# Two more trees for k's maximum, a new list of all steps, and the two-input chain carried on to batch 6

## The chip, the core and the metric

The kernel runs on one core of a Trainium2 chip. A core has five engines that work through queues of their own and wait for one another through semaphores: TensorE (PE, matrix products), VectorE (DVE), ScalarE (ACT), GpSimd (POOL) and SyncE (SP, which here only issues transfers). The metric is the device time of one launch in microseconds, as the median of several runs; lower is better.

## The reference

Attention with two softmaxes feeds a feed-forward block with a product in its middle. There are 8 batches of 8 heads, 576 tokens and 64 channels in each head; the feed-forward block has 4608 tokens, 512 channels and 1024 hidden columns.

```python
q_s = softmax(q, axis=-1)            # over the 64 channels, eps 1e-9 in the divisor
k_s = softmax(k, axis=2)             # over the 576 tokens
kv  = einsum('bhsd,bhse->bhde', k_s, v)
x   = einsum('bhsd,bhde->bhse', q_s, kv)   # then tokens x (heads * channels)
out = ((x @ w1) * (x @ w2)) @ w3 @ w_out
```

Each softmax subtracts its maximum before the exponential, as `np.max` and `np.exp` in the reference do.

## The kernel before, in words

`w3 @ w_out` is folded into one matrix first (`fold`): `w3t` transposes a block of w3 on TensorE, `w3T` copies it out of PSUM, `pf` multiplies it with w_out in two halves, `W3O` scales the result into SBUF. Fillers (`FILL`, line 350) keep TensorE busy at the start.

The eight batches of attention (`attention(b)`) each run these steps. For k: `kmx` is the maximum over the nine token groups that a partition holds; `cb` carries it across the partitions; `ksub` subtracts it (in two halves, by heads), `kexp` takes the exponential, `vc` casts v (batches 0 and 1 load v cast already), `kv` is the product, `kv2` divides by the sums and moves it out of PSUM. For q, in two parts of four and five token groups: `qmx` maximum, `qsub`, `qexp`, `qsm` sum, `qeps` and `qrc` (1e-9 added, reciprocal), `qn` product, then a transpose: `qt` and `qT` through TensorE for batches 0 and 1, `qd` by a transposing transfer from batch 2 on. `xm` and `xt` multiply both, `xs` and `xts` move the result to SBUF as x.

The feed-forward block (`chunk(c)`) takes the tokens of one batch at a time (chunks 0 to 7 the first 512, chunk 8 the last 64 of every batch). `up.1` and `up.0` are the products with w2 and w1, `bs` copies the first out of PSUM, `ab` multiplies both (VectorE), `down` multiplies with the folded matrix, `os` copies out, `st` stores. Chunks 0 and 1 are cut into two halves of 256 tokens. The number behind a name is batch or chunk, then half, block, or part: `up.0.0.1.2` is the w1 product of chunk 0, half 1, block 2.

The maximum `kmx` has two forms. `kmx_one` (line 481) is one reduce on VectorE for each half of the heads. `kmx_tree` (line 488) is four two-input maxima on whole tiles, 4, 2, 1 and 1 token groups wide. `TREES` (line 310) is the number of batches, from 0 on, that use the tree.

What runs on which engine is written out in `PICKS`, and the order on every engine in `ORDER`: the steps are emitted in that order, so each engine's queue is its share of the list. `LOADS` is the order of transfers issued by GpSimd, `LATE` of those by SyncE, which also issues `st` and `qd`. A load waits for the landing of the one eight places ahead of it in its queue, and for the buffer that it fills. PSUM is cut into rings: four banks for `up` (`pab`), two for `down` (`po`), two for attention (`att`). An `up` that finds its ring full waits for the `bs` or `ab` that frees the oldest bank.

Two-input steps of GpSimd and of VectorE (`pairs`, `kmx_tree`, `qeps` of VectorE, `vc` of GpSimd) are marked `port`. Among the first `LINKED` steps of the list, a marked step waits for the marked step ahead of it in the list if that one is on the other engine:

```python
if s["port"] and i < LINKED:
    assert got, name
    if held and held[0] != s["eng"]:
        link(got[0], held[1])
    held = s["eng"], got[-1]
```

Of the kernel before, what the change touches and what calls it, by code (L numbers as in the profile page):

```python
# [101 lines left out]
os.1.3 up.1.2.0.2 up.0.2.0.2 bs.2.0.2 qrc.3.0 ab.2.0.1 qn.3.0 kexp.3.0 up.1.2.0.3 ab.2.0.2  # L102
up.0.2.0.3 kmx.4.1 bs.2.0.3 kv.3 qd.3.0 up.1.2.0.4 ab.2.0.3 up.0.2.0.4 vc.5.0 vc.5.1 vc.4.1 vc.4.0
k.5 st.1.3 st.0.3 st.1.1 v.6 v.7 bs.2.0.4 kv2.3 os.1.2 up.1.2.0.5 ab.2.0.4 st.1.2 up.0.2.0.5
bs.2.0.5 qmx.4.0 xt.2 xm.3.1 xts.2.0 up.1.2.0.6 xts.2.1 ab.2.0.5 qsub.4.0 xs.3.1.1 xm.3.0 bs.2.0.6
xt.3 up.0.2.0.6 xts.3.1 xs.3.0.0 cb.4 up.1.2.0.7 xts.3.0 xs.3.0.1 up.0.2.0.7 xs.3.1.0 bs.2.0.7
ab.2.0.6 up.1.3.0.0 ksub.4.0 qexp.4.0 ab.2.0.7 down.2.0 kmx.5.1 bs.3.0.0 down.2.1 ksub.4.1 kexp.4.0
qmx.5.1 up.0.3.0.0 os.2.0 up.1.3.0.1 qsub.5.1 kexp.4.1 ab.3.0.0 down.2.2 qmx.5.0 bs.3.0.1 kmx.5.0
qsub.5.0 up.0.3.0.1 qeps.4.1 up.1.3.0.2 up.0.3.0.2 qrc.4.1 os.2.1 ab.3.0.1 qn.4.1 up.1.3.0.3 qsm.4.0
k.6 st.2.1 down.2.3 bs.3.0.2 qeps.4.0 ab.3.0.2 qexp.5.1 qd.4.1 up.0.3.0.3 qrc.4.0 qn.4.0 bs.3.0.3  # L110
st.2.0 up.1.3.0.4 qsm.5.1 kv.4 bs.3.0.4 ab.3.0.3 up.0.3.0.4 qd.4.0 qexp.5.0 os.2.2 up.1.3.0.5
ab.3.0.4 q.6 st.2.2 up.0.3.0.5 kv2.4 bs.3.0.5 qeps.5.1 up.1.3.0.6 os.2.3 qrc.5.1 ab.3.0.5 qn.5.1
up.0.3.0.6 st.2.3 bs.3.0.6 xm.4.0 ab.3.0.6 xm.4.1 xs.4.0.0 xt.4 up.1.3.0.7 xs.4.1.1 up.0.3.0.7
xs.4.1.0 bs.3.0.7 xs.4.0.1 ab.3.0.7 down.3.0 cb.5 down.3.1 os.3.0 xts.4.1 st.3.0 xts.4.0 kmx.6.0
ksub.5.0 up.1.4.0.0 os.3.1 down.3.2 bs.4.0.0 st.3.1 q.7 kmx.6.1 ksub.5.1 qd.5.1 up.0.4.0.0 kexp.5.0
up.1.4.0.1 qsm.5.0 up.0.4.0.1 bs.4.0.1 ab.4.0.0 qeps.5.0 up.1.4.0.2 kexp.5.1 ab.4.0.1 up.0.4.0.2
qrc.5.0 bs.4.0.2 qmx.6.1 qn.5.0 up.1.4.0.3 os.3.2 vc.6.0 up.0.4.0.3 st.3.2 ab.4.0.2 up.1.4.0.4
# [791 lines left out]
```

## Time and profile before

| | |
|---|---|
| median of 3 runs | 242.06 us (242.03 to 242.16) |
| the profiled execution | 242.07 us, of which the span is 240.3 us |
| granted TensorE clock | 1.00 |
| busy: TensorE, VectorE, ScalarE, GpSimd | 232.4, 182.0, 118.5, 110.2 us |
| transfers issued by SyncE, by GpSimd | 34.22 MB, 11.14 MB |

The span runs from the first to the last instruction of the profile. Each row of a timeline gives the start, the length, the engine (PEld is TensorE's loading of weights, which runs beside its products), the line of the kernel, the operation with the tiles it writes and reads, and, in brackets, how long the engine stood idle before it and what ended that wait. An instruction's length includes some 0.1 us in which the next one already runs, so the distance of starts tells what an instruction costs its engine. Times of matmul ends are modelled.

```profile
DVE  2949798989899899989689999997756335535530
```

This row has the busy tenths of VectorE in 40 slices of 6 us each.

### The profile page before, as it was taken

How to read it: one execution, taken by the hardware profiler on the slowest of the kernel's cores; microseconds unless marked ns; L12 is line 12 of the kernel's file. 1: busy time of each engine (PE TensorE's matmuls, PEld its weight loads, DVE VectorE, ACT ScalarE, POOL GpSimd, SP SyncE). 2: the span in 40 equal slices, each digit the busy share in tenths (PEclk: the TensorE clock that was granted, in tenths of full speed). 3: DMA queues.
4: the chain of work that ended last, by engine and by line, in shares of the span. 5: the costliest groups of instructions: out<-in, count | busy, mean ns of one | idle time of the engine just before them, and what ended most of it. 6: DMA issues, size and time to landing. Idle time of an engine off the chain costs nothing.

```text
span 240.3 us, 4954 instructions
## 1 busy us (share of the span) xinstructions
PE 232.4 (97%) x1987; PEld 121.0 (50%) x1987; DVE 182.0 (76%) x306; ACT 118.5 (49%) x187; POOL 110.2 (46%) x73
## 2 busy tenths in 40 slices
...
DVE  2949798989899899989689999997756335535530
...
GB/s 203 217 305 209 324 222 296 235 393 391 314 261 277 402 217 194 323 372 284 206 232 213 260 125 0 57 151 68 65 124 87 46 0 0 0 132 1 131 131 131
DMA packets 37894, 45.66 MB, mean 190 GB/s; under 512 B 15984, under 2 KB 22384, under 8 KB 37872
## 3 DMA queue, kind: packets, MB, share of 16 engines
q1 hardware_dynamic: 30080, 34.22, 50.3%
q0 software_dynamic: 7792, 11.14, 21.1%
...
## 4 chain that ended last, share of the span: by engine, by line
PE 83%; DVE 6%; DMA 6%; issue 2%; POOL 1%; ACT 1%; DVEq 0%; POOLq 0%
PE pab L768 50%; PE po L790 23%; DMA k<-in_k_dram 6%; PE po L805 3%; PE pkv L540 2%; PE po L452 2%; PE xm L654 2%; DVE ab L783 1%; DVE k L515 1%; DVE km L484 1%; PE qtp L621 1%; POOL w L402 1%; PE po L654 1%; DVE mx L506 1%; DVE kmx L493 1%
## 5 line engine op out<-in xcount | busy, mean ns | idle before, releaser
L783 DVE TENSOR_TENSOR ab<-pab,bsb 128x512 f16<-128x512 f32 x72 | 48.7, 682 | 24.0 <-PE pab L768 19.7
L768 PE MATMUL pab<-x,w2sb 128*128 128x512 f16 (+1 forms) x320 | 66.0, 337 | 0.0
L768 PE MATMUL pab<-x,w1sb 128*128 128x512 f16 (+1 forms) x320 | 65.9, 337 | 0.0
L323 ACT CAST bsb<-pab 128x512 f16<-128x512 f32 x59 | 34.5, 587 | 54.3 <-PE pab L768 53.9
L790 PE MATMUL po<-W3O,ab 128*128 128x512 f16 x256 | 59.7, 379 | 1.2 <-DVE ab L783 1.2
L768 PEld LDWEIGHTS <-w1sb 128*128 128x128 f16 x352 | 33.9, 98 | 27.6 <-DMA w1sb<-in_moe_w_dram 0.2
L768 PEld LDWEIGHTS <-w2sb 128*128 128x128 f16 x352 | 33.4, 98 | 27.6 <-issue 1.3
L790 PEld LDWEIGHTS <-ab 128*128 128x128 f16 x256 | 24.7, 98 | 30.6 <-DVE ab L783 1.9
L515 POOL TENSOR_TENSOR k<-k,cb 128x1152 f32<-128x1152 f32 x12 | 31.4, 2636 | 14.9 <-DVE cb L511 8.4
L574 POOL TENSOR_TENSOR q<-q,qm 128x1024 f32<-128x1024 f32 (+1 forms) x14 | 29.7, 2125 | 12.8 <-DVE qm L569 12.7
L606 POOL TENSOR_TENSOR en<-eq,qr 128x1280 f16<-128x1280 f16 (+1 forms) x12 | 25.8, 2159 | 20.7 <-DVE qr L599 20.7
L484 DVE TENSOR_REDUCE km<-k 128x128 f32<-128x1152 f32 x12 | 25.9, 2166 | 0.0
L569 DVE TENSOR_REDUCE qm<-q 128x20 f32<-128x1280 f32 (+1 forms) x16 | 21.3, 1342 | 3.6 <-DMA q<-in_q_dram 3.6
L523 ACT ACTIVATE ek<-k 128x1152 f16<-128x1152 f32 x16 | 18.5, 1163 | 9.5 <-POOL k L515 8.8
L323 ACT COPY osb<-po 128x512 f32<-128x512 f32 (+1 forms) x22 | 12.7, 576 | 20.6 <-PE po L790 14.1
L323 DVE COPY osb<-po 128x512 f32<-128x512 f32 (+1 forms) x15 | 10.0, 668 | 15.4 <-PE po L790 9.7
L587 DVE TENSOR_REDUCE qr<-eq 128x20 f32<-128x1280 f16 (+1 forms) x16 | 21.3, 1341 | 0.5 <-ACT eq L582 0.5
L582 ACT ACTIVATE eq<-q 128x1280 f16<-128x1280 f32 (+1 forms) x16 | 18.8, 1174 | 5.6 <-POOL q L574 3.8
L452 PE MATMUL po<-wosb,w3T 128*128 128x512 f16 x64 | 15.5, 379 | 0.7 <-DMA wosb<-in_moe_w_out_dram 0.4
L327 ACT ACTIVATE x<-xm 128x512 f16<-128x512 f32 x18 | 10.4, 608 | 4.6 <-PE xm L654 4.6
L323 DVE CAST bsb<-pab 128x512 f16<-128x512 f32 x13 | 8.9, 687 | 2.8 <-PE pab L768 2.3
L350 PE MATMUL po<-zero 128*128 128x512 f16 x31 | 9.2, 458 | 1.6 <-DVE zero L345 1.6
...
## 6 DMA issues: line engine op xcount, KB each, us to landing
...
q<-in_q_dram SPq DMA_DIRECT2D x6, 1152.0 KB, 6.8
v<-in_v_dram SPq DMA_DIRECT2D x6, 1152.0 KB, 10.0
k<-in_k_dram SPq DMA_DIRECT2D x5, 1152.0 KB, 6.8
k<-in_k_dram POOLq DMA_DIRECT2D x3, 1152.0 KB, 14.2
...
```

The lines of the kernel that those rows point to most:

```text
L323: return [(nc.scalar.copy if eng == "ACT" else engine[eng].tensor_copy)(out=out, in_=in_)]
L452: nc.tensor.matmul(st["pf", ft], lhsT=st["w3T", ft][:, gt, :], rhs=wosb[:, gt, :], start=(gt == 0), stop=(gt == N_FT - 1))
L484: dve.tensor_reduce(out=st["km", b][:, two(hp), :], in_=kb[:, two(hp), :, :].rearrange("p h j d -> p h d j"), axis=AX.X, op=ALU.max)
L515: return [engine[eng].tensor_tensor(out=kb[:, two(hp), :, :], in0=kb[:, two(hp), :, :], in1=st["cb", b][:, two(hp), None, :].broadcast_to( ...
L569: dve.tensor_reduce(out=st["qm", b][:, :, j], in_=qb[:, :, j, :], axis=AX.X, op=ALU.max)
L574: return [engine[eng].tensor_tensor(out=qb[:, :, j, :], in0=qb[:, :, j, :], in1=st["qm", b][:, :, j, None].broadcast_to([P, HH, n, D]), op ...
L582: nc.scalar.activation(out=st["eq", b, p], in_=qb[:, :, j, :], func=AF.Exp)
L587: dve.tensor_reduce(out=st["qr", b][:, :, slice(*PARTS[p])], in_=st["eq", b, p], axis=AX.X, op=ALU.add)
L606: return [engine[eng].tensor_tensor(out=st["en", b][:, j, :, :].rearrange("p j h d -> p h j d"), in0=st["eq", b, p], in1=st["qr", b][:, :, ...
L768: nc.tensor.matmul(st["p", one, c, sub, u][:, a * (t1 - t0):(a + 1) * (t1 - t0)], lhsT=w[:, ct, fb * P:(fb + 1) * P], rhs=x()[:, ct, t0:t1 ...
L783: dve.tensor_tensor(out=st["ab", c][:, nf * u:nf * u + nf, t0:t1], in0=cut(st["p", 0, c, sub, u]), in1=cut(st["bsb", c, sub, u]), op=ALU.mult)
L790: nc.tensor.matmul(st["po", c, tb], lhsT=st["ab", c][:, ft, tb * P:(tb + 1) * P], rhs=W3O[:, ft, :], start=(ft == 0), stop=(ft == N_FT - 1))
```

## The change

The change does four things. `TREES` goes from 2 to 4, so `kmx.2.0` and `kmx.3.0` are trees, and `kmx.2.1` and `kmx.3.1` fall away. `LINKED` goes from 350 to 559, which reaches into batch 6's products. `ORDER` and `PICKS` are written anew for every engine. `LOADS` and `LATE` follow: row 1 of w3 is loaded ahead of `k.0`, and `v.0` behind `w3.2` and `q.1.0`; SyncE's loads of batches 3 to 7 change places among themselves and with the stores.

```diff
-LINKED = 350
+LINKED = 559
 
 ORDER = """
-q.0.1 q.0.0 qmx.0.1 qsub.0.1 w3.3 w3.4 qexp.0.1 qmx.0.0 wo.0 wo.1 k.0 ident qsub.0.0 qexp.0.0 w3t.3
-w3t.4 w3t.5 w3T.3 qsm.0.1 w3T.4 qeps.0.1 qrc.0.1 w3.0 w3.1 pf.3.0 qn.0.1 pf.4.0 qt.0.16 pf.3.1 W3O.3
-w3T.5 pf.4.1 qt.0.8 w3.5 v.0 w3.2 q.1.0 qT.0.8 W3O.4 pf.5.0 w3t.0 k.1 w3T.0 pf.5.1 w2.0 W3O.5 w3t.1
-pf.0.0 qT.0.16 w3T.1 pf.0.1 W3O.0 w3t.7 w3T.7 pf.1.0 w3t.6 pf.7.0 pf.1.1 w1.0 qsm.0.0 qeps.0.0
-kmx.0.0 cb.0 ksub.0.1 kexp.0.1 w1.1 ksub.0.0 qrc.0.0 kexp.0.0 kv.0 qn.0.0 kv2.0 w3t.2 pf.7.1 qt.0.0
-w2.1 qmx.1.0 W3O.1 w3T.6 k.2 W3O.7 w3T.2 pf.6.0 w2.2 qT.0.0 xm.0.0 xs.0.0.1 qsub.1.0 w1.2 qexp.1.0
-kmx.1.0 pf.6.1 pf.2.0 pf.2.1 xs.0.0.0 xm.0.1 xs.0.1.0 xs.0.1.1 up.1.0.0.0 up.0.0.0.0 up.1.0.1.0
-bs.0.0.0 up.0.0.1.0 up.1.0.0.1 w2.3 qsm.1.0 qeps.1.0 ab.0.0.0 qrc.1.0 w1.3 up.0.0.0.1 cb.1 qn.1.0
-v.1 ksub.1.0 q.1.1 ksub.1.1 qt.1.0 W3O.2 bs.0.1.0 ab.0.1.0 up.1.0.1.1 up.0.0.1.1 bs.0.0.1 W3O.6
-qT.1.0 bs.0.1.1 ab.0.0.1 q.2 v.2 kmx.2.0 ab.0.1.1 xt.0 kexp.1.0 up.1.0.0.2 bs.0.0.2 up.0.0.0.2
-up.1.0.1.2 up.0.0.1.2 kmx.2.1 ab.0.0.2 cb.2 ksub.2.0 ksub.2.1 xts.0.0 xts.0.1 up.1.0.0.3 up.0.0.0.3
-bs.0.0.3 ab.0.0.3 down.0.0 kexp.1.1 bs.0.1.2 ab.0.1.2 kv.1 kv2.1 down.0.1 xm.1.0 qmx.1.1 xs.1.0.0
-os.0.0 kexp.2.0 xs.1.0.1 up.1.0.1.3 up.0.0.1.3 up.1.1.0.0 up.0.1.0.0 bs.0.1.3 kexp.2.1 qsub.1.1
-qmx.2.0 qsub.2.0 bs.1.0.0 os.0.1 qexp.1.1 qmx.2.1 ab.0.1.3 vc.2.1 vc.2.0 down.0.2 up.1.1.0.1
-qexp.2.0 qsub.2.1 ab.1.0.0 qsm.1.1 qeps.1.1 bs.1.0.1 up.0.1.0.1 up.1.1.0.2 kv.2 k.3 v.3 st.0.0 q.3
-qsm.2.0 qeps.2.0 qrc.1.1 qn.1.1 qexp.2.1 ab.1.0.1 up.0.1.0.2 up.1.1.0.3 up.0.1.0.3 qrc.2.0 kv2.2
-bs.1.0.3 os.0.2 qsm.2.1 qt.1.16 qt.1.8 qeps.2.1 bs.1.0.2 ab.1.0.3 qrc.2.1 qT.1.16 ab.1.0.2 qn.2.0
-down.0.3 qn.2.1 qT.1.8 xm.1.1 vc.3.0 xs.1.1.1 xs.1.1.0 q.4 down.1.0 qd.2.0 kmx.3.0 qd.2.1 qmx.3.0
-xt.1 vc.3.1 up.1.1.1.0 up.0.1.1.0 up.1.1.1.1 bs.1.1.0 up.0.1.1.1 up.1.1.1.2 xts.1.0 bs.1.1.1 os.1.0
-xts.1.1 kmx.3.1 ab.1.1.0 os.0.3 qmx.3.1 xm.2.0 qsub.3.0 qmx.4.1 ab.1.1.1 qsub.3.1 qsub.4.1
-up.0.1.1.2 down.1.1 xs.2.0.1 bs.1.1.2 k.4 st.0.1 v.5 v.4 st.0.2 xs.2.0.0 xm.2.1 xs.2.1.1 xs.2.1.0
-up.1.1.1.3 up.0.1.1.3 up.1.2.0.0 bs.1.1.3 qexp.3.1 ab.1.1.2 cb.3 ksub.3.0 ksub.3.1 up.0.2.0.0
-ab.1.1.3 kmx.4.0 bs.2.0.0 qexp.3.0 q.5 qsm.3.1 os.1.1 qexp.4.1 qsm.3.0 qeps.3.0 ab.2.0.0 qeps.3.1
-qrc.3.1 qn.3.1 qd.3.1 st.1.0 qsm.4.1 kexp.3.1 up.1.2.0.1 bs.2.0.1 up.0.2.0.1 down.1.2 down.1.3
...
+q.0.1 qmx.0.1 q.0.0 qsub.0.1 qmx.0.0 qexp.0.1 w3.3 w3.4 wo.0 wo.1 w3.1 ident qsub.0.0 w3t.3 w3T.3
+k.0 w3.0 w3t.4 qsm.0.1 qexp.0.0 qeps.0.1 qrc.0.1 w3T.4 w3t.5 pf.3.0 pf.4.0 qsm.0.0 qeps.0.0 pf.3.1
+W3O.3 w3.5 w3.2 q.1.0 qn.0.1 qt.0.8 pf.4.1 w3t.1 qrc.0.0 w3T.5 v.0 k.1 w2.0 qn.0.0 qt.0.16 pf.5.0
+w3T.1 W3O.4 qT.0.8 pf.5.1 kmx.0.0 cb.0 qt.0.0 w3t.0 W3O.5 ksub.0.1 w3T.0 pf.1.0 pf.1.1 pf.0.0 W3O.1
+ksub.0.0 w3t.7 pf.0.1 w3T.7 qT.0.0 qT.0.16 kexp.0.1 W3O.0 w3t.2 pf.7.0 w3t.6 w3T.2 qmx.1.0 kexp.0.0
+pf.7.1 w1.0 W3O.7 qsub.1.0 pf.2.0 w1.1 w2.1 k.2 w3T.6 kv.0 kv2.0 pf.2.1 qexp.1.0 xm.0.0 qsm.1.0
+xs.0.0.1 pf.6.0 pf.6.1 xs.0.0.0 qeps.1.0 xm.0.1 xs.0.1.0 up.1.0.0.0 xs.0.1.1 up.0.0.0.0 up.1.0.1.0
+w2.2 kmx.1.0 qrc.1.0 w1.2 cb.1 w2.3 w1.3 v.1 qn.1.0 bs.0.0.0 up.0.0.1.0 up.1.0.0.1 ab.0.0.0 W3O.2
+qt.1.0 ksub.1.0 q.1.1 up.0.0.0.1 bs.0.1.0 up.1.0.1.1 bs.0.0.1 ab.0.1.0 qT.1.0 xt.0 ab.0.0.1 bs.0.1.1
+kmx.2.0 up.0.0.1.1 up.1.0.0.2 ab.0.1.1 up.0.0.0.2 up.1.0.1.2 up.0.0.1.2 xts.0.0 xts.0.1 kexp.1.0
+bs.0.0.2 ab.0.0.2 up.1.0.0.3 up.0.0.0.3 bs.0.1.2 up.1.0.1.3 ksub.1.1 cb.2 q.2 kexp.1.1 ab.0.1.2
+up.0.0.1.3 v.2 W3O.6 bs.0.0.3 ab.0.0.3 kv.1 down.0.0 ksub.2.0 bs.0.1.3 kexp.2.0 kv2.1 ksub.2.1
+xm.1.0 os.0.0 xs.1.0.1 xs.1.0.0 qmx.1.1 ab.0.1.3 kexp.2.1 down.0.1 qmx.2.0 qsub.1.1 up.1.1.0.0
+up.0.1.0.0 up.1.1.0.1 up.0.1.0.1 qsub.2.0 vc.2.0 down.0.2 qmx.2.1 bs.1.0.0 qexp.1.1 os.0.1 vc.2.1
+qexp.2.0 ab.1.0.0 qsm.1.1 bs.1.0.1 qeps.1.1 qsm.2.0 qsub.2.1 os.0.2 qrc.1.1 qn.1.1 ab.1.0.1 qeps.2.0
+kv.2 up.1.1.0.2 up.0.1.0.2 up.1.1.0.3 kv2.2 qrc.2.0 up.0.1.0.3 qt.1.16 qt.1.8 down.0.3 qexp.2.1
+qsm.2.1 bs.1.0.3 bs.1.0.2 qn.2.0 qeps.2.1 ab.1.0.3 ab.1.0.2 qrc.2.1 st.0.0 k.3 q.3 v.3 st.0.2 qT.1.8
+qd.2.0 qn.2.1 st.0.1 qd.2.1 k.4 qT.1.16 xm.1.1 xs.1.1.0 xs.1.1.1 down.1.0 xt.1 qmx.3.1 up.1.1.1.0
+qmx.3.0 kmx.3.0 up.0.1.1.0 up.1.1.1.1 os.0.3 up.0.1.1.1 bs.1.1.0 bs.1.1.1 cb.3 qsub.3.0 down.1.1
+xts.1.1 xts.1.0 os.1.0 qexp.3.0 xm.2.0 ab.1.1.1 qsub.3.1 ab.1.1.0 xs.2.0.1 xs.2.0.0 up.1.1.1.2
+up.0.1.1.2 qsm.3.0 xm.2.1 qexp.3.1 xs.2.1.0 xs.2.1.1 bs.1.1.2 ab.1.1.2 qsm.3.1 up.1.1.1.3 up.0.1.1.3
+bs.1.1.3 ab.1.1.3 up.1.2.0.0 up.0.2.0.0 up.1.2.0.1 qeps.3.1 vc.3.0 kmx.4.0 bs.2.0.0 up.0.2.0.1
+ab.2.0.0 qeps.3.0 bs.2.0.1 qrc.3.0 ksub.3.1 ksub.3.0 kexp.3.0 q.4 kexp.3.1 up.1.2.0.2 up.0.2.0.2
+up.1.2.0.3 vc.3.1 os.1.1 qrc.3.1 ab.2.0.1 kmx.4.1 qmx.4.1 kv.3 down.1.2 up.0.2.0.3 qn.3.0 kv2.3 xt.2
+bs.2.0.3 bs.2.0.2 qmx.4.0 ab.2.0.2 os.1.2 st.0.3 v.4 q.5 qd.3.0 qn.3.1 up.1.2.0.4 down.1.3
+up.0.2.0.4 qsub.4.1 qd.3.1 qexp.4.1 ab.2.0.3 xts.2.1 xts.2.0 os.1.3 xm.3.0 xm.3.1 xt.3 bs.2.0.4
+qsm.4.1 ab.2.0.4 qeps.4.1 xts.3.0 xs.3.0.1 xts.3.1 xs.3.0.0 up.1.2.0.5 bs.2.0.5 xs.3.1.1 xs.3.1.0
+qsub.4.0 vc.4.0 cb.4 ksub.4.1 up.0.2.0.5 up.1.2.0.6 up.0.2.0.6 qexp.4.0 ab.2.0.5 ksub.4.0 up.1.2.0.7
+up.0.2.0.7 qrc.4.1 qmx.5.1 bs.2.0.6 ab.2.0.6 vc.4.1 k.5 st.1.1 up.1.3.0.0 up.0.3.0.0 st.1.3 qsm.4.0
+st.1.2 st.1.0 v.5 bs.2.0.7 qmx.5.0 ab.2.0.7 up.1.3.0.1 kexp.4.1 qeps.4.0 kexp.4.0 bs.3.0.0 qrc.4.0
+kmx.5.1 down.2.0 up.0.3.0.1 kv.4 kmx.5.0 qn.4.1 os.2.0 vc.5.1 bs.3.0.1 v.6 qd.4.1 qn.4.0 qsub.5.0
+cb.5 down.2.1 os.2.1 down.2.2 down.2.3 os.2.2 ab.3.0.0 kv2.4 up.1.3.0.2 qd.4.0 xm.4.0 os.2.3 xm.4.1
...
 LOADS = [
-    ("w3", 3), ("w3", 4), ("wo", 0), ("wo", 1), ("k", 0), ("w3", 0), ("w3", 1), ("w3", 5), ("v",
-    0), ("w3", 2), ("q", 1, 0), ("k", 1), ("w2", 0), ("w1", 0), ("w1", 1), ("w2", 1), ("k", 2),
-    ("w2", 2), ("w1", 2), ("w2", 3), ("w1", 3), ("v", 1), ("q", 1, 1),
+    ("w3", 3), ("w3", 4), ("wo", 0), ("wo", 1), ("w3", 1), ("k", 0), ("w3", 0), ("w3", 5),
+    ("w3", 2), ("q", 1, 0), ("v", 0), ("k", 1), ("w2", 0), ("w1", 0), ("w1", 1), ("w2", 1),
+    ("k", 2), ("w2", 2), ("w1", 2), ("w2", 3), ("w1", 3), ("v", 1), ("q", 1, 1),
 ]
...
 LATE = [
-    ("q", 2), ("v", 2), ("k", 3), ("v", 3), ("q", 3), ("q", 4), ("k", 4), ("v", 5), ("v", 4),
-    ("q", 5), ("k", 5), ("v", 6), ("v", 7), ("k", 6), ("q", 6), ("q", 7), ("k", 7),
+    ("q", 2), ("v", 2), ("k", 3), ("q", 3), ("v", 3), ("k", 4), ("q", 4), ("v", 4), ("q", 5),
+    ("k", 5), ("v", 5), ("v", 6), ("q", 6), ("k", 6), ("v", 7), ("q", 7), ("k", 7),
 ]
...
-    TREES = 2
+    TREES = 4
```

Of `PICKS`, the steps that change engine up to chunk 2: to VectorE go `qsub.0.0` and `ksub.2.0` (from GpSimd), `w3T.2`, `w3T.5`, `W3O.2`, `W3O.6`, `W3O.7`, `qT.0.8`, `os.0.1`, `os.1.2`, `bs.1.1.2` and `xts.2.1` (from ScalarE); from VectorE go `bs.0.0.3`, `bs.0.1.2`, `xts.0.0`, `xts.2.0`, `xs.1.0.0`, `os.0.0`, `os.1.3`, `w3T.3`, `qT.1.16` and the `qeps` of batches 0 and 1 to ScalarE, `qn.0.0` to GpSimd; `vc.2.0` and `vc.3.1` go from ScalarE to GpSimd and `vc.2.1` the other way. Later on, the parts of `q` that VectorE multiplies are `qn.6.1` and `qn.7.1` instead of `qn.4.0` and `qn.7.0`, `ksub.6.0` and `ksub.7.0` go to GpSimd, and the copies `bs`, `os` and `xs` are shared out differently between VectorE and ScalarE.

Beyond these lines, `st.3.3` stands behind `qd.7.0` in the new list, and `os.4.3` behind both.

88 lines of the change are left out of this document (40 added, 48 removed), and 97 rows, old and new, of the table PICKS.

## The prediction

> **What bounds the kernel now.** I read the busy rows first, then the waits of TensorE, then its stretches, then the timelines of TensorE, VectorE and GpSimd, and last the chain. The first two say that TensorE is the bound: it is busy for 97% of the span and waits for little.
>
> ```profile
> PE 232.4 (97%) x1987; PEld 121.0 (50%) x1987; DVE 182.0 (76%) x306; ACT 118.5 (49%) x187; POOL 110.2 (46%) x73
> ```
>
> ```profile
> PE po L350 <- DVE zero L345: 1.6, 1, 1.6
> PE po L790 <- DVE ab L783: 1.2, 1, 1.2
> ```
>
> The start (1.6) is not touched. What is left is 1.2 us at one matmul of `down`; the other rows of that view are shorter and lie in the folding of the weights. The stretches tell where nothing is to be had: from 66 to 100 and from 135 to 186 us TensorE is full, and between them (columns: length, then busy time of PE, PEld, DVE, ACT, POOL), though VectorE is idle for only 34.00 - 32.55 = 1.45 us of the first of them.
>
> ```profile
> 66.00:100.00 34.00, 34.00 (x298) 18.15 (x296) 32.55 (x53) 25.56 (x45) 25.90 (x14) 1.00 0.95 281
> ...
> 135.00:186.00 51.00, 51.00 (x457) 23.48 (x442) 42.06 (x77) 26.39 (x45) 20.95 (x10) 1.00 0.43 96
> ```
>
> TensorE's timeline shows the one late place:
>
> ```profile
> 43.31 1.05 PE L768 MATMUL pab<-x,w1sb 128*128 128x256 f16 x8
> ...
> 47.69 1.46 PE L790 MATMUL po<-W3O,ab 128*128 128x512 f16 x6
> 50.37 0.60 PE L790 MATMUL po<-W3O,ab 128*128 128x512 f16 x2 [1.23 <-DVE ab L783]
> 50.91 0.78 PE L540 MATMUL pkv<-v,ek 64*64 64x64 f16 x72
> ...
> 52.15 1.90 PE L790 MATMUL po<-W3O,ab 128*128 128x512 f16 x8
> ...
> 74.82 0.41 PE L654 MATMUL xm<-qT,kv 64*64 64x512 f16 x4
> 75.17 1.05 PE L768 MATMUL pab<-x,w1sb 128*128 128x256 f16 x8
> ```
>
> `down.0.0` starts at 47.69, does six matmuls, and waits 1.23 us for `ab.0.0.3`. The first row there is `up.0.0.0.2`, and the weight loads show why it starts at 43.31: its columns of w1 have just landed.
>
> ```profile
> 43.30 0.77 PEld L768 LDWEIGHTS <-w1sb 128*128 128x128 f16 x8 [0.24 <-DMA w1sb<-in_moe_w_dram]
> ```
>
> **The change, part by part.** The sum is made against the profiled execution, 242.07 us for a span of 240.3; the median of the runs is 242.06, so it stands for them, and the 1.77 us outside the span stay.
>
> *Up to 43.3 us: nothing.* Both lists have the same TensorE steps ahead of `up.0.0.0.2` (folds, products, transposes, fillers), so what moves within them can't be gained while the w1 columns (0.24 above) come when they do. They come from GpSimd's load queue, which lands in order. The load of row 1 of w3 now stands ahead of `k.0`, `v.0` behind `w3.2` and `q.1.0`, but the bytes ahead of `w1.2` are the same. If the landing were earlier, the gain is at most that 0.24.
>
> *What pays for that order is `k.0`.* Its own transfer and work in the chain, and the queue (each issue waits for an older landing, named at the right):
>
> ```profile
> 3.76 14.24 DMA k<-in_k_dram
> ...
> 23.23 2.64 DVE k L515 x2
> ...
> 83.59 3.45 PE po L790 x16
> 87.04 3.45 PE pab L768 x16
> ...
> 237.03 0.37 ACT osb L323
> ```
>
> ```profile
> 19.38 0.75 POOL L402 DMA_DIRECT2D w1sb<-in_moe_w_dram  x1 [0.35 <-DMA w<-in_moe_w_dram]
> 20.62 0.74 POOL L402 DMA_DIRECT2D w1sb<-in_moe_w_dram  x1 [0.49 <-DMA w<-in_moe_w_dram]
> ...
> 29.58 0.74 POOL L402 DMA_DIRECT2D w1sb<-in_moe_w_dram  x1 [0.74 <-DMA q<-in_q_dram]
> ...
> 40.29 2.65 POOL L515 TENSOR_TENSOR k<-k,cb 128x1152 f32<-128x1152 f32 x1
> ...
> 48.83 5.21 POOL L515 TENSOR_TENSOR k<-k,cb 128x1152 f32<-128x1152 f32 x2 [2.50 <-DVE cb L511]
> ...
> 62.92 6.50 POOL L606 TENSOR_TENSOR en<-eq,qr 128x1280 f16<-128x1280 f16 x3 [0.55 <-DVE qr L599]
> ```
>
> Rows `w3.0` and `w3.1` land 20.62 - 19.38 = 1.24 us apart, so `k.0` lands at 18.0 + 1.24 = 19.2. `v.0` becomes the last of its set, at about 29.4 (the third row). TensorE's new list has `w3t.2`, `pf.7.1`, `qt.0.0` and `pf.2.0` ahead of `kv.0`, so it doesn't stand idle long. VectorE is what `k.0` delays:
>
> ```profile
> 28.45 0.23 DVE L559 TENSOR_SCALAR rc<-pkv 128x2 f32<-128x2 f32 x2 [1.18 <-PE pkv L550]
> ...
> 29.33 1.21 DVE L569 TENSOR_REDUCE qm<-q 128x16 f32<-128x1024 f32 x1
> 30.46 0.68 DVE L323 COPY qT<-qtp 128x1024 f16<-128x1024 f16 x1
> 31.05 1.22 DVE L574 TENSOR_TENSOR q<-q,qm 128x1024 f32<-128x1024 f32 x1
> 32.26 1.23 DVE L493 TENSOR_TENSOR kmx<-k 128x1024 f32<-128x1024 f32 x1
> ...
> 35.05 1.21 DVE L587 TENSOR_REDUCE qr<-eq 128x16 f32<-128x1024 f16 x1
> ...
> 37.21 0.24 DVE L599 RECIPROCAL qr<-qr 128x16 f32<-128x16 f32 x1
> ...
> 39.51 0.65 DVE L783 TENSOR_TENSOR ab<-pab,bsb 128x512 f16<-128x512 f32 x1
> ...
> 41.12 2.17 DVE L484 TENSOR_REDUCE km<-k 128x128 f32<-128x1152 f32 x1
> ...
> 49.62 0.69 DVE L783 TENSOR_TENSOR ab<-pab,bsb 128x512 f16<-128x512 f32 x1
> ```
>
> From `k.0` to the end of its two `ksub` is 23.23 + 2.64 - 18.0 = 7.9 us: 27.1. Then, by this list, three moves at 0.59 (30.46 to 31.05), `qmx.1.0` 1.13, `qsub.1.0` 1.21: 31.2. `kv2.0` 0.88: 32.1. `qsm.1.0` 1.21: 33.3. `kmx.1.0`, a tree, takes 35.05 - 32.26 = 2.79: 36.1. Reciprocal and `cb.1` 39.51 - 37.21 = 2.30: 38.4. Now the longer chaining: `kmx.2.0` is a tree, so it waits for `ksub.1.0` of GpSimd, 2.65: 41.1; the `ab` steps listed in between fill that wait. The tree 2.79: 43.9; `ab.0.1.1` 0.7: 44.6. It frees the bank that `up.0.0.1.2` takes at 43.31 + 2 x 0.86 = 45.0 (87.04: four `up` in 3.45). **Slack 0.4 us.** Behind the waiting tree on VectorE stand `ab.0.1.1`, `ab.0.0.2` and `cb.2`, and through the banks TensorE.
>
> *The tree of batch 2* replaces two reduces of 2.17 by 2.79: 1.5 us less on VectorE just ahead of the late `ab.0.0.3`. `bs.0.0.3`, `bs.0.1.2` and `xts.0.0` go to ScalarE (half idle); `W3O.2` and `W3O.6` come in, two moves of 0.6. *The new order* helps more: `up.1.0.1.3`, `up.0.0.1.3` (0.86 each) and `kv.1` (52.15 - 50.91 = 1.24) go ahead of `down.0.0`, which then needs `ab.0.0.3` at about 47.69 + 3.0 + 1.3 (its six matmuls) = 52.0, where the old VectorE order ended it at 49.62 + 0.69 = 50.3. The new one, after the 44.6 above, has `ab.0.0.2`, `cb.2`, `ab.0.1.2` and `W3O.6` ahead of it and ends it at 44.6 + 2.3 + 4 x 0.6 = 49.3. Gain: the whole 1.23 us.
>
> *The tree of batch 3* has the second new wait: `kmx.3.0` waits for `qn.2.1`, the last of GpSimd's batch-2 work. That work begins after `ksub.2.0`, which VectorE now does, by 49.3 + 1.3 = 50.6. The old rows run from 48.83 to 62.92 + 6.50 = 69.42, 20.6 us; without one `ksub` (2.6) this is 18.0, so `qn.2.1` ends at about 68.6. `qmx.3.1` and `qmx.3.0` fill VectorE meanwhile. Then tree 2.79, `cb.3` 2.3, two `ab` 1.3: 75.0. They free the bank of `up.0.1.1.2`, which started at 75.17 and now has `down.1.1` (3.45 / 2) ahead of it: 75.17 - 1.23 + 1.73 = 75.7. Slack 0.7.
>
> *SP's queue.* `st.0.0` now stands ahead of `k.3`, `q.3` and `v.3`, so these wait for `down.0.0` (52.4) and its copy. `k.3` lands near 53 + 1.2 + 6.8 = 61, and `kmx.3.0` asks for it at 68.6. `xm.2.0`, near 74.4, needs the transpose `qd.2.1`, issued behind `qn.2.1` and `st.0.1`: 68.6 + 3.6, with some 2 us to spare. `st.3.3` stands behind `qd.7.0`, and `os.4.3` of VectorE behind it, in a stretch where VectorE has 8.9 of 51 us free. No cost.
>
> ```profile
> k<-in_k_dram SPq DMA_DIRECT2D x5, 1152.0 KB, 6.8
> ...
> qT<-en SPq DMA_TRANSPOSE x12, 3.6
> ```
>
> *From there to `down.2.0`* the list asks VectorE for ten `ab`, two reduces over k (batch 4 keeps them), one `cb`, seven reduces over q or its exponentials, one `kv2` and some small steps.
>
> ```profile
> L569 DVE TENSOR_REDUCE qm<-q 128x20 f32<-128x1280 f32 (+1 forms) x16 | 21.3, 1342 | 3.6 <-DMA q<-in_q_dram 3.6
> ```
>
> With 0.08 us of overlap between neighbours: 6.1 + 4.2 + 2.3 + 7 x 1.26 + 0.9 + 1.2 = 23.5 us. TensorE has 19 `up` at 3.45 / 4 and two split ones (18.1), two `down` (3.45), `kv.3` (0.7) and six products (three at 75.17 - 74.82 = 0.35, the others shorter; some 1.4): 23.7. Slack 0.2, if VectorE never idles. Later batches have the same rows with more room, and from 186 us on nothing but matmuls; the end (the last copy at 237.03, then its store) is the same.
>
> The price of slacks as thin as these isn't in the trace. Its bounds: nothing, since each sum still closes; and the 3.3 us of the chain below. I take 0.2, near the lower end, because each sum closes with rows that waited in their own right. **Sum: 242.07 - 1.23 + 0.2 = 241.0.**
>
> A rule speaks against trees. The Trainium skill (SBUF — State Buffer, Who interferes with whom) says that a VectorE instruction with two SBUF inputs shuts out a GpSimd instruction that reads SBUF, one of them blocked whole, while `tensor_reduce` never contends. The trace agrees: above, the reduce at 41.12 takes 2.17 beside GpSimd's 40.29 to 42.94, but here
>
> ```profile
> 169.62 2.34 POOL L606 TENSOR_TENSOR en<-eq,qr 128x1280 f16<-128x1280 f16 x1 [1.54 <-DVE qr L599]
> ```
>
> ```profile
> 171.34 1.70 DVE L606 TENSOR_TENSOR en<-eq,qr 128x1024 f16<-128x1024 f16 x1
> ```
>
> VectorE's product of 1.22 (31.05's size) takes 1.70 while GpSimd runs until 171.96. By that rule each tree also costs GpSimd 2.79 us; after the first, `ksub.1.1` ends at 46.6, `kv.1` is due at 49.4, so the sum stays.
>
> **Rivals.** *The room goes (no change).* VectorE idles 1.45 us again between `up.0.1.1.2` and `down.2.0`: 1.2 beyond the slack, 241.0 + 1.2 = 242.2. The same comes if `k.0` lands a two-row load later. For it: VectorE's 96% there. Against: the same share made TensorE wait nowhere before.
>
> *The chain makes VectorE wait (slower).* Place: `kmx.3.0` behind `qn.2.1`. From 69.3 on each us is one of TensorE's. If GpSimd's two last products wait for their reciprocals as such products did before (20.7 us over 9, 2.3 each)
>
> ```profile
> POOL en L606 <- DVE qr L599: 20.7, 9, 7.1
> ```
>
> `qn.2.1` ends at 50.6 + 17.4 (20.6 less the `ksub` and the 0.55 that the last row waited) + 4.6 = 72.6, 3.3 too late: 244.3. It decides from about 70.8 on, where the gain is gone. For it: VectorE never waited for GpSimd in the old list, and now does five times (`kmx.2.0`, `ksub.2.0`, `kmx.3.0`, `qeps.5.0`, `qeps.6.1`). Against: the reciprocals stand close ahead in the new list, and chained work can't collide.
>
> *The change does nothing*: `ab.0.0.3` just comes later too, 242.1. Against: three more us of cover.
>
> **How the numbers follow.** Forecast 0.56; no room or no effect 0.18; the chain 0.26. A difference under 0.2% (0.5 us) can't be told from no change; so faster 0.56, same 0.18, slower 0.26. The likeliest case alone runs from 240.6 (all of 1.23 and 0.24) to 241.5; the range, with the rivals' nearer parts, from 240.5 to 243.4.
>
> **What would show it.** Right: no wait for `ab` at L790, `down.0.0` running through; TensorE at 43.3 in `up.0.0.0.2` with the w1 wait; stretches after 66 us full; the last copy starting near 236.0. Wrong: TensorE idle for `ab` near 45, 76 or 100 us, VectorE's L493 waiting for GpSimd L515 or L606 for over half a us, or `k.0` landing after 20.

## The result and the profile after

The changed kernel takes 240.61 us in the median of four runs (240.45 to 241.06), the kernel before 242.11 us beside it. The ratio is 0.994, with a 95% interval of 0.9923 to 0.9957: faster by 1.5 us, at the lower edge of the forecast case of 240.6 to 241.5. The profiled execution took 240.74 us, with a span of 239.0. Line numbers of the code are smaller by one than before (L767 is `up`, L782 `ab`, L789 `down`, L492 to L495 the tree).

First the busy row of the page, then the whole of TensorE's waits (us in total, times, longest), then two of the stretches (columns as before).

```profile
PE 231.4 (97%) x1987; PEld 121.4 (51%) x1987; DVE 180.8 (76%) x312; ACT 116.4 (49%) x185; POOL 110.2 (46%) x73
```

```profile
PE w3t L439 <- DMA w<-in_moe_w_dram: 2.1, 2, 1.8
PE po L349 <- DVE zero L344: 1.6, 1, 1.6
PE po L451 <- DMA wosb<-in_moe_w_out_dram: 0.5, 1, 0.5
```

```profile
66.00:100.00 34.00, 34.00 (x295) 18.09 (x294) 32.87 (x56) 25.03 (x45) 26.82 (x13) 1.00 1.00 283
...
135.00:186.00 51.00, 51.00 (x399) 23.47 (x398) 40.74 (x70) 21.68 (x36) 20.08 (x10) 1.00 0.32 66
```

The 1.2 us for `ab` are gone, and no other wait for VectorE has come in their place. What is new is 1.8 us for a block of w3 in the folding, before 43 us. TensorE's timeline, at the places that the prediction named:

```profile
43.61 1.04 PE L767 MATMUL pab<-x,w1sb 128*128 128x256 f16 x8
...
48.85 1.04 PE L767 MATMUL pab<-x,w1sb 128*128 128x256 f16 x8
49.82 0.78 PE L539 MATMUL pkv<-v,ek 64*64 64x64 f16 x72
...
51.06 1.90 PE L789 MATMUL po<-W3O,ab 128*128 128x512 f16 x8
...
75.80 1.04 PE L767 MATMUL pab<-x,w1sb 128*128 128x256 f16 x8
...
100.55 1.89 PE L789 MATMUL po<-W3O,ab 128*128 128x512 f16 x8
```

`down.0.0` (51.06) runs its eight matmuls through. VectorE and GpSimd beside it:

```profile
19.39 1.23 DVE L492 TENSOR_TENSOR kmx<-k 128x1024 f32<-128x1024 f32 x1 [1.97 <-DMA k<-in_k_dram]
...
41.58 1.22 DVE L492 TENSOR_TENSOR kmx<-k 128x1024 f32<-128x1024 f32 x1
...
44.36 1.28 DVE L782 TENSOR_TENSOR ab<-pab,bsb 128x512 f16<-128x512 f32 x2
...
47.73 0.65 DVE L782 TENSOR_TENSOR ab<-pab,bsb 128x512 f16<-128x512 f32 x1
...
48.91 0.68 DVE L782 TENSOR_TENSOR ab<-pab,bsb 128x512 f16<-128x512 f32 x1
...
68.70 1.22 DVE L492 TENSOR_TENSOR kmx<-k 128x1024 f32<-128x1024 f32 x1
...
73.80 1.25 DVE L782 TENSOR_TENSOR ab<-pab,bsb 128x512 f16<-128x512 f32 x2
...
100.23 0.68 DVE L782 TENSOR_TENSOR ab<-pab,bsb 128x512 f16<-128x512 f32 x1
```

```profile
22.21 0.74 POOL L401 DMA_DIRECT2D w1sb<-in_moe_w_dram  x1 [1.82 <-DMA w<-in_moe_w_dram]
...
38.79 2.62 POOL L514 TENSOR_TENSOR k<-k,cb 128x1152 f32<-128x1152 f32 x1 [0.23 <-DVE cb L510]
...
44.53 2.62 POOL L514 TENSOR_TENSOR k<-k,cb 128x1152 f32<-128x1152 f32 x1 [2.37 <-DVE km L495]
...
66.33 2.34 POOL L605 TENSOR_TENSOR en<-eq,qr 128x1280 f16<-128x1280 f16 x1 [0.75 <-DVE qr L598]
```

Neither tree waits for GpSimd (no bracket at 41.58 or 68.70). It is GpSimd that waits: `ksub.1.1` stands idle 2.37 us until the first tree is done.

Where the time went: from `up.0.0.0.2` to the last copy out, the kernel before took 237.03 - 43.31 = 193.72 us, this one 235.72 - 43.61 = 192.11 (the row below).

```profile
235.72 0.37 ACT L322 COPY osb<-po 128x256 f32<-128x256 f32 x1 [1.21 <-PE po L804]
```

Of the 1.61 us, the wait is 1.38 by starts: 50.37 - (47.69 + 6 x 0.216), with 3.45/16 us for one matmul of `down`. The remaining 0.23 fits a count of the starts: where products of 128 rows and of 64 follow each other, 20 distances of some 0.31 us stood before and 18 stand now, 0.1 more than the usual 0.216 each (the same 0.1 shows at 49.82, which starts 0.97 after its neighbour where 0.87 is usual). That last part was counted, not tried. Against it, `up.0.0.0.2` starts 0.30 later in this execution.

### The profile page after: what moved, and what is told of

The parts are those of the page before. It is cut to its first block, busy times and chain, and to the rows that moved or that the text cites. A ratio compares the mean times of both kernels' runs of the same rounds, so it can differ in the third digit from the quotient of the medians.

```text
span 239.0 us, 4957 instructions
## 1 busy us (share of the span) xinstructions
PE 231.4 (97%) x1987; PEld 121.4 (51%) x1987; DVE 180.8 (76%) x312; ACT 116.4 (49%) x185; POOL 110.2 (46%) x73
## 4 chain that ended last, share of the span: by engine, by line
PE 89%; DMA 7%; POOL 2%; issue 0%; ACT 0%; ACTq 0%; POOLq 0%
PE pab L767 53%; PE po L789 23%; DMA w<-in_moe_w_dram 7%; PE po L451 4%; PE po L804 3%; PE pkv L539 2%; PE xm L653 2%; PE w3t L439 1%; POOL w L401 1%; PE po L653 0%; PE pkv L549 0%; PE qtp L620 0%; POOL wosb L401 0%; POOL k L401 0%; PE xt L653 0%
## 5 line engine op out<-in xcount | busy, mean ns | idle before, releaser
L767 PE MATMUL pab<-x,w2sb 128*128 128x512 f16 (+1 forms) x320 | 66.0, 337 | 0.0
L767 PE MATMUL pab<-x,w1sb 128*128 128x512 f16 (+1 forms) x320 | 65.9, 337 | 0.0
L782 DVE TENSOR_TENSOR ab<-pab,bsb 128x512 f16<-128x512 f32 x72 | 48.5, 679 | 22.2 <-PE pab L767 20.1
L789 PE MATMUL po<-W3O,ab 128*128 128x512 f16 x256 | 59.4, 379 | 0.0
L322 ACT CAST bsb<-pab 128x512 f16<-128x512 f32 x52 | 30.2, 587 | 45.4 <-PE pab L767 38.4
L767 PEld LDWEIGHTS <-w1sb 128*128 128x128 f16 x352 | 34.1, 98 | 27.3
L767 PEld LDWEIGHTS <-w2sb 128*128 128x128 f16 x352 | 33.5, 98 | 27.3 <-issue 0.7
L605 POOL TENSOR_TENSOR en<-eq,qr 128x1024 f16<-128x1024 f16 (+1 forms) x13 | 26.8, 2075 | 28.1 <-issue 19.3
L789 PEld LDWEIGHTS <-ab 128*128 128x128 f16 x256 | 24.6, 98 | 29.0 <-issue 0.4
L514 POOL TENSOR_TENSOR k<-k,cb 128x1152 f32<-128x1152 f32 x13 | 34.0, 2625 | 11.0 <-DVE k L514 3.8
L322 ACT COPY osb<-po 128x512 f32<-128x512 f32 (+1 forms) x25 | 14.4, 577 | 34.9 <-PE po L789 27.6
L573 POOL TENSOR_TENSOR q<-q,qm 128x1280 f32<-128x1280 f32 (+1 forms) x13 | 27.7, 2142 | 7.5 <-DVE qm L568 4.1
L322 DVE COPY osb<-po 128x512 f32<-128x512 f32 (+1 forms) x12 | 8.0, 667 | 15.5 <-PE po L789 8.3
L483 DVE TENSOR_REDUCE km<-k 128x128 f32<-128x1152 f32 x8 | 17.2, 2161 | 0.0
L322 DVE CAST bsb<-pab 128x512 f16<-128x512 f32 x20 | 13.7, 686 | 3.9 <-PE pab L767 3.6
L326 ACT ACTIVATE x<-xm 128x512 f16<-128x512 f32 x21 | 11.9, 603 | 3.2 <-PE xm L653 3.2
```

What stands on the lines that cost most here:

```text
L322: return [(nc.scalar.copy if eng == "ACT" else engine[eng].tensor_copy)(out=out, in_=in_)]
L514: return [engine[eng].tensor_tensor(out=kb[:, two(hp), :, :], in0=kb[:, two(hp), :, :], in1=st["cb", b][:, two(hp), None, :].broadcast_to( ...
L573: return [engine[eng].tensor_tensor(out=qb[:, :, j, :], in0=qb[:, :, j, :], in1=st["qm", b][:, :, j, None].broadcast_to([P, HH, n, D]), op ...
L605: return [engine[eng].tensor_tensor(out=st["en", b][:, j, :, :].rearrange("p j h d -> p h j d"), in0=st["eq", b, p], in1=st["qr", b][:, :, ...
L767: nc.tensor.matmul(st["p", one, c, sub, u][:, a * (t1 - t0):(a + 1) * (t1 - t0)], lhsT=w[:, ct, fb * P:(fb + 1) * P], rhs=x()[:, ct, t0:t1 ...
L782: dve.tensor_tensor(out=st["ab", c][:, nf * u:nf * u + nf, t0:t1], in0=cut(st["p", 0, c, sub, u]), in1=cut(st["bsb", c, sub, u]), op=ALU.mult)
```

## The experiments

They ran in three groups of four, each beside the kernel before, whose medians there were 242.31, 242.24 and 242.31 us. Between groups, and with the changed kernel (ratio 0.994), only ratios are compared.

**The order alone.** The kernel before, with TensorE's three steps put ahead of `down.0.0` and three copies given to ScalarE.

```diff
-bs.0.0.3 ab.0.0.3 down.0.0 kexp.1.1 bs.0.1.2 ab.0.1.2 kv.1 kv2.1 down.0.1 xm.1.0 qmx.1.1 xs.1.0.0
-os.0.0 kexp.2.0 xs.1.0.1 up.1.0.1.3 up.0.0.1.3 up.1.1.0.0 up.0.1.0.0 bs.0.1.3 kexp.2.1 qsub.1.1
+bs.0.0.3 ab.0.0.3 kexp.1.1 bs.0.1.2 up.1.0.1.3 ab.0.1.2 up.0.0.1.3 kv.1 down.0.0 kv2.1 down.0.1
+xm.1.0 qmx.1.1 xs.1.0.0 os.0.0 kexp.2.0 xs.1.0.1 up.1.1.0.0 up.0.1.0.0 bs.0.1.3 kexp.2.1 qsub.1.1
```

> The kernel before, with reduces and the short chain; only up.1.0.1.3, up.0.0.1.3 and kv.1 go ahead of down.0.0, and bs.0.0.3, bs.0.1.2, xts.0.0 go to ScalarE. Theory 1 (the gain is the order of TensorE around down.0.0, trees are not needed for it): no wait for ab at L790, 1.2 to 1.5 us under before, about 240.8. Theory 2 (the gain is the VectorE time that the tree of batch 2 saves): the wait moves to up.0.0.1.3 or down.0.0 and stays at 0.8 us or more, 241.6 or above.

Measured: 243.33 us, ratio 1.004 (1.0026 to 1.0054). TensorE's waits for VectorE in it:

```profile
PE pab L768 <- DVE ab L783: 0.8, 1, 0.8
PE pab L768 <- DVE x L329: 0.8, 1, 0.8
PE po L790 <- DVE ab L783: 0.5, 1, 0.5
```

The wait at `down.0.0` is taken away and comes back as 0.8 us in `up.0.0.1.3`, which now comes before its bank is free, and as two others after it. VectorE is rid of three copies here (0.25, 0.67 and 0.68 us), but both reduces of batch 2, and `cb.2` behind them, still stand ahead of the `ab` that `up.0.0.1.3` asks for. So the order alone only moves the place where TensorE meets VectorE.

**The trees alone, chained.** The kernel before with two more trees; `kmx.2.1` and `kmx.3.1` fall out of the list.

```diff
-    TREES = 2
+    TREES = 4
```

> The kernel before, with trees for batches 2 and 3 at the old places of the first reduce, and the chain of 350 as it is. In this list kmx.2.0 stands behind ksub.1.1, so it waits for GpSimd until 46.3 instead of starting at 41.1. Theory 1: ab.0.1.1 ends near 49.8 instead of 43.9, TensorE asks for its bank at 45.0, so 4 to 5 us of waiting against 1.2 saved: 245 to 246. Theory 2: the 1.5 us saved on VectorE count, 240.8 to 241.2.

Measured: 246.78 us, ratio 1.0183 (1.0151 to 1.0215). In the old list `ksub.1.1` stands ahead of `kmx.2.0`, so the chained tree waits for two steps of GpSimd, and TensorE for the `ab` behind the tree. TensorE's timeline and one of its stretches (length, busy time, granted clock, share of DMA, GB/s):

```profile
50.15 1.87 PE L768 MATMUL pab<-x,w2sb 128*128 128x256 f16 x8 [3.87 <-DVE ab L783]
51.82 1.81 PE L768 MATMUL pab<-x,w1sb 128*128 128x256 f16 x8
```

```profile
50.00:53.00 3.00, 2.85 (x14) 0.50 1.05 390
```

The wait of 3.87 us isn't all. The granted clock is 0.50 for the next 3 us, and two `up` take 1.67 and 1.64 us from start to start where 0.87 is usual: 1.57 us more.

**The trees alone, unchained from the first new tree on.** As the last one, and the chain ends just ahead of `kmx.2.0`.

```diff
-LINKED = 350
+LINKED = 130
...
-    TREES = 2
+    TREES = 4
```

> As the run before, but the chain ends ahead of kmx.2.0, so that trees and GpSimd's two-input steps may meet. If they shut each other out whole (a product beside GpSimd took 1.70 us instead of 1.22): the tree at 41.1 ends about 1.8 to 2.6 us later than its 2.8 alone, that is at 45.7 to 46.5, where the two reduces ended at 45.9: no change, 241.8 to 242.6. If they hardly disturb each other: the tree ends at 43.9 and the wait at down.0.0 goes, 240.8.

Measured: 247.38 us, ratio 1.021 (1.0181 to 1.024). The timelines of VectorE and of GpSimd say why:

```profile
41.37 6.26 DVE L493 TENSOR_TENSOR kmx<-k 128x1024 f32<-128x1024 f32 x1
```

```profile
40.54 2.63 POOL L515 TENSOR_TENSOR k<-k,cb 128x1152 f32<-128x1152 f32 x1
...
43.91 2.63 POOL L515 TENSOR_TENSOR k<-k,cb 128x1152 f32<-128x1152 f32 x1
```

The tree's first step of 1.22 us lasts 6.26. It begins under one `ksub` and ends 1.09 us after the other, about its own length; GpSimd's steps keep their 2.63. Without the chain the tree pays more than the whole of what it meets, and the time lies above both expectations.

**The new list without the new trees.** The changed kernel with two reduces in place of each new tree (`kmx.2.1` and `kmx.3.1` right behind their first halves).

```diff
-LINKED = 559
+LINKED = 561
...
-    TREES = 4
+    TREES = 2
```

> The changed kernel with the two reduces in place of each tree of batches 2 and 3, at the same places; all else as changed. The reduces take 1.4 us more of VectorE and wait for nothing. Theory 1 with the slack as forecast (0.4 us at up.0.0.1.2, 0.7 us at up.0.1.1.2): TensorE waits 0.6 to 1.0 us near 45 and 0.3 to 0.7 us near 76, 241.4 to 242.2. If trees are of no use to the new list: 240.6.

Measured: 242.35 us, ratio 1.0002 (0.998 to 1.0025): the whole gain is lost. TensorE waits for `ab` near 49 us (0.57, in `up.0.0.1.3`) and near 84 (0.24), and near 112 for a copy of VectorE's; none of it is at the two places that theory 1 named:

```profile
PE pab L767 <- DVE ab L782: 0.8, 2, 0.6
PE xm L653 <- DVE bsb L322: 0.8, 1, 0.8
```

**The chain ending where it did.** The changed kernel with the old end of the chain.

```diff
-LINKED = 559
+LINKED = 350
```

> The changed kernel with the chain between VectorE and GpSimd beginning where it did in the kernel before, so that only the new part of the chain ahead of that point is gone, trees and lists as changed. Theory 1 (the new part of the chain only fixes an order that both engines keep anyway, since ksub.1.0 ends before kmx.2.0 begins): same time as the changed kernel, 240.5 to 240.8 us. Theory 2 (the chain is what keeps the first tree from running beside ksub): kmx.2.0 runs beside ksub.1.0 and takes up to the 6.3 us that it took unchained in the kernel with the old lists, a wait of 2 us or more near 45 in up.0.0.1.2: 242.5 to 244.

The text above has the edit the wrong way round: `LINKED` is where the chain ends. What goes is the chain from the load `k.5` on, behind both new trees. Measured: 240.49 us, ratio 0.9923 (0.9904 to 0.9943), which can't be told from the changed kernel. The longer chain itself shows neither a gain nor a cost.

**No chain at all.**

```diff
-LINKED = 559
+LINKED = 0
```

> The changed kernel without any chain between VectorE's and GpSimd's two-input steps. Theory 1 (the chain sets the price of a tree: unchained, a tree step that meets a GpSimd step runs 1.2 us to 6.3 us): waits of TensorE at the tree of batch 2 or 3, near 45 and 76, one to four us: 242 to 246 us. Theory 2 (the order of the new lists keeps tree and ksub apart by themselves): 240.4 to 240.9, and the tree's first steps at 1.22 us.

Measured: 246.06 us, ratio 1.0148 (1.0126 to 1.017). The first tree starts in time, but `ksub.1.1` no longer waits for it, and its second step, of 0.69 us, runs beside it. VectorE's timeline, then GpSimd's:

```profile
41.34 1.22 DVE L492 TENSOR_TENSOR kmx<-k 128x1024 f32<-128x1024 f32 x1
42.59 2.99 DVE L493 TENSOR_TENSOR kmx<-kmx 128x512 f32<-128x512 f32 x1
...
71.70 2.28 DVE L493 TENSOR_TENSOR kmx<-kmx 128x512 f32<-128x512 f32 x1
74.01 2.44 DVE L494 TENSOR_TENSOR kmx<-kmx 128x256 f32<-128x256 f32 x1
```

```profile
42.22 2.81 POOL L514 TENSOR_TENSOR k<-k,cb 128x1152 f32<-128x1152 f32 x1
...
70.61 5.57 POOL L573 TENSOR_TENSOR q<-q,qm 128x1024 f32<-128x1024 f32 x2
```

The second tree meets two `qsub`. Its second and third steps take 2.28 and 2.44 us for 0.69 and 0.42, and here GpSimd pays too: 5.57 us for the two steps that take 4.20 in the changed kernel. TensorE waits for `ab` four times, 2.8 us in all, first in `up.1.0.0.3`:

```profile
47.15 1.03 PE L767 MATMUL pab<-x,w2sb 128*128 128x256 f16 x8 [1.00 <-DVE ab L782]
```

The list alone doesn't keep the engines apart. Against the kernel with the old end of the chain (240.49 us in the same group), the chain up to `k.5` is worth 5.6 us here, for all the steps that it orders and not for the trees alone.

**`down.0.0` back ahead of the three steps**, all else as changed.

```diff
-bs.0.0.2 ab.0.0.2 up.1.0.0.3 up.0.0.0.3 bs.0.1.2 up.1.0.1.3 ksub.1.1 cb.2 q.2 kexp.1.1 ab.0.1.2
-up.0.0.1.3 v.2 W3O.6 bs.0.0.3 ab.0.0.3 kv.1 down.0.0 ksub.2.0 bs.0.1.3 kexp.2.0 kv2.1 ksub.2.1
+bs.0.0.2 ab.0.0.2 up.1.0.0.3 up.0.0.0.3 bs.0.1.2 ksub.1.1 cb.2 q.2 kexp.1.1 ab.0.1.2 v.2 W3O.6
+bs.0.0.3 ab.0.0.3 down.0.0 kv.1 up.1.0.1.3 up.0.0.1.3 ksub.2.0 bs.0.1.3 kexp.2.0 kv2.1 ksub.2.1
```

> The changed kernel with down.0.0 put back ahead of kv.1, up.1.0.1.3 and up.0.0.1.3, all else as changed. Theory 1 (the trees make VectorE early enough, the new place of down.0.0 adds little): TensorE gets to down.0.0 near 49.3, ab.0.0.3 ends at 49.6 or sooner, a wait of 0 to 0.4 us at most in down.0.0: 240.6 to 241.0 us. Theory 2 (the new place of down.0.0 is what takes the wait away, as the prediction put it): the wait of 1.2 us comes back, 241.7 to 241.9 us.

Measured: 241.36 us, ratio 0.9966 (0.9946 to 0.9987), between the two theories. TensorE waits again in `down.0.0`, for less than before the change:

```profile
49.46 0.60 PE L789 MATMUL po<-W3O,ab 128*128 128x512 f16 x2 [0.36 <-DVE ab L782]
```

By ratios the new place is worth 0.6 us, but the intervals of this kernel and of the changed one overlap a little. Within the group it is 0.87 us, against 240.49 for the kernel with the old end of the chain, and all eight runs of this one are slower than all six of that one. Of this, the row above explains 0.36; the rest was not traced.

**The old start.** Lists, engines and loads of the kernel before up to `up.1.0.1.0`, from there those of the changed one.

```diff
-    ("w3", 3), ("w3", 4), ("wo", 0), ("wo", 1), ("w3", 1), ("k", 0), ("w3", 0), ("w3", 5),
+    ("w3", 3), ("w3", 4), ("wo", 0), ("wo", 1), ("k", 0), ("w3", 0), ("w3", 1), ("w3", 5), ("v",
...
```

> The list of work and of loads as in the kernel before up to up.1.0.1.0, and as in the changed one from there; trees and chain as changed. Theory 1 (the changed start costs TensorE 0.3 us, by the wait for w3.0 at w3t.0, and nothing comes back for it): up.0.0.0.2 at 43.3 and not 43.6, the waits of w3t under 0.5 us, 240.2 to 240.5 us. Theory 2 (the changed start is what gives kmx.2.0 and ab.0.1.1 their room of 0.4 us near 45): a wait of 0.3 to 1.3 us in up.0.0.1.2, 240.7 to 241.9 us.

Measured: 240.78 us, ratio 0.9939 (0.9919 to 0.9959). Neither theory's mechanism shows: `up.0.0.0.2` starts at 43.43 (43.61 in the changed kernel), there is no wait for `ab`, and the time is the same. The new start neither gains nor costs, because two things cancel in it. VectorE's first step on `k.0` starts earlier with the old start than with the new one (19.39 in the changed kernel):

```profile
18.26 1.23 DVE L492 TENSOR_TENSOR kmx<-k 128x1024 f32<-128x1024 f32 x1 [2.91 <-DMA k<-in_k_dram]
```

But `up.0.0.0.2` comes 43.43 - 18.26 = 25.17 us behind that step here, and 23.94 or 23.95 us behind it in seven of the nine kernels with the new start (24.22 in the other two, one of them the changed kernel). So the new start loads `k.0` some 1.1 us later and is 1.2 us shorter from there.

**The tree of batch 2 alone, and the tree of batch 3 alone.** `TREES = 3` for the first; for the second, the edit below. The two reduces come back in the other batch.

```diff
-    TREE = [b < TREES for b in range(B)]
+    TREE = [b < TREES and b != 2 for b in range(B)]
```

> The changed kernel with the tree in batch 2 alone; batch 3 has its two reduces back (1.45 us more of VectorE, and no step that waits for qn.2.1). Theory 1 (the two trees pay for different waits, and that of batch 3 keeps VectorE from being late after 100 us, where the kernel without both trees waited for 1.1 us in two products): 241.5 to 241.8 us, no wait before 100. Theory 2 (the prediction's thin sum of 0.2 us up to down.2.0 holds): a wait of about 1.2 us before 100 us: 241.6 to 242.0, and it stands near 76 or at 100. Theory 3 (TensorE has room there): 240.4 to 240.8.

> The changed kernel with the tree in batch 3 alone; batch 2 has its two reduces back (1.45 us more of VectorE ahead of ab.0.1.1 and ab.0.0.3). Theory 1 (the tree of batch 2 pays for the wait near 49, of 0.6 us in the kernel without both trees, and nothing else): 241.0 to 241.4 us, the one wait for ab in up.0.0.1.3. Theory 2 (lateness of VectorE there is carried on to later products): 241.6 to 242.3, with waits after 66 too.

Measured: 241.55 us, ratio 0.9972 (0.9959 to 0.9985), with only the tree of batch 2; 241.64 us, ratio 0.9975 (0.9965 to 0.9985), with only that of batch 3. By ratios, against the changed kernel, that is 0.8 us each, and both missing cost 1.5. So each tree pays for about half. The missing tree of batch 2 shows in `up.0.0.1.3` of the second kernel, the one wait for `ab` that theory 1 named, at a higher price than it gave:

```profile
49.77 1.03 PE L767 MATMUL pab<-x,w1sb 128*128 128x256 f16 x8 [0.57 <-DVE ab L782]
```

The missing tree of batch 3 costs 0.24 us for an `ab` at 83.5 in the first kernel, which no theory named, and then waits for late transposes of q, near 111 and 134:

```profile
PE xm L653 <- DMA qT<-en: 1.4, 2, 0.8
```

These 1.4 us are from the slowest of its twelve runs (240.74 to 242.54), which is the one profiled; how the loss is made up in the others stays open.

**0.73 us more in the first tree, and 0.73 us more in the second.** The second maximum is done twice (for the other kernel with `b == 3`).

```diff
+                *(top(out=t[:, :, 0:2, :], in0=t[:, :, 0:2, :], in1=t[:, :, 2:4, :], op=ALU.max)
+                  for _ in range(int(b == 2))),
```

> The changed kernel with one more VectorE step of 0.73 us within the tree of batch 2, which repeats its second maximum and changes no value. Theory 1 (the slack near 45 is the 0.36 us between the end of ab.0.1.1 and the start of up.0.0.1.2): a wait of 0.3 to 0.4 us in up.0.0.1.2, 240.9 to 241.1 us. Theory 2 (there is more room than the rows show): no wait, 240.4 to 240.8. Theory 3 (one late step is made later by those behind it): two waits or more, 241.2 to 242.

> The changed kernel with one more VectorE step of 0.73 us within the tree of batch 3, which repeats its second maximum and changes no value. Theory 1 (0.75 us of slack near 76, but only 0.2 us from there to down.2.0, as the prediction summed it): no wait near 76, some 0.5 us of waits by 102, 241.0 to 241.2 us. Theory 2 (VectorE's idle time of 1.1 us between 66 and 100 is room that it can use): no wait, 240.4 to 240.8.

Measured: in the first tree 241.5 us, ratio 0.9973 (0.9957 to 0.999); in the second 240.73 us, ratio 0.9936 (0.9907 to 0.9964).

In the first tree the whole of it comes through, but not where the prediction had the thin place. Timelines of TensorE, VectorE and ScalarE:

```profile
45.55 1.04 PE L769 MATMUL pab<-x,w1sb 128*128 128x256 f16 x8
...
49.94 1.03 PE L769 MATMUL pab<-x,w1sb 128*128 128x256 f16 x8 [0.73 <-ACT bsb L322]
```

```profile
45.43 1.28 DVE L784 TENSOR_TENSOR ab<-pab,bsb 128x512 f16<-128x512 f32 x2
```

```profile
48.25 1.16 ACT L524 ACTIVATE ek<-k 128x1152 f16<-128x1152 f32 x1 [1.91 <-POOL k L516]
49.32 1.05 ACT L322 CAST bsb<-pab 128x512 f16<-128x512 f32 x2
```

`up.0.0.1.2` starts at 45.55 while `ab.0.1.1` (45.43) still runs, so it doesn't take that bank. The wait is in `up.0.0.1.3` (49.94), for a copy of ScalarE that stands behind `kexp.1.1`, which waited 1.91 us for `ksub.1.1`, which the chain holds behind the tree. So the tree also reaches TensorE through GpSimd and ScalarE. In this kernel that matmul waits for ScalarE's semaphore, in the changed kernel for VectorE's, so the two kernels take different banks there, and the length of the path differs.

In the second tree nothing comes through. TensorE is full from 66 to 100 us, and VectorE is busy for 33.30 us of them instead of 32.87:

```profile
66.00:100.00 34.00, 34.00 (x295) 18.07 (x294) 33.30 (x56) 24.45 (x44) 27.05 (x13) 1.00 0.98 288
```

This kernel also has the changed start, and its `up.0.0.0.2` starts at 43.22, its load at 20.59 instead of 22.21:

```profile
20.59 0.74 POOL L401 DMA_DIRECT2D w1sb<-in_moe_w_dram  x1 [0.32 <-DMA w<-in_moe_w_dram]
```

So the 1.8 us for w3 belong to single executions (that of the changed kernel and that with only the tree of batch 3), not to the list. They also move `up.0.0.0.2` by only 0.28 us: it comes 24.22 us behind VectorE's first step on `k.0` there, and 43.22 - 19.28 = 23.94 here.

```profile
19.28 1.22 DVE L492 TENSOR_TENSOR kmx<-k 128x1024 f32<-128x1024 f32 x1 [1.97 <-DMA k<-in_k_dram]
```

## Why the prediction was right, point by point

*What bounds the kernel, and the gain.* Right. The one late place is gone, and its 1.23 us (1.38 by starts) are the gain.

*Up to 43.3 us, nothing.* Right in size, by luck: the old start under the new rest gives the same time, but the reason was wrong. The prediction held that TensorE can't be earlier than the columns of w1, and that `k.0` delays only VectorE. No wait for w1 stands in the trace after. What `up.0.0.0.2` follows is `k.0`: it began between 43.19 and 43.81 in the nine kernels with this start, as VectorE's first step on `k.0` began between 19.25 and 19.87. That the later `k.0` costs nothing is due to the way from there, which the new list makes 1.2 us shorter; the prediction has no term for that.

*k.0 and the walk from it.* The steps came as worked out: `k.0` at 19.3 for 19.2 (VectorE's row at 19.39), `ksub.1.0` done at 38.79 + 2.62 = 41.4 for 41.1, the two `ab` from 44.36 on, so `ab.0.1.1` done near 45.0 for 44.6. Wrong is what it was held against: `up.0.0.1.2` doesn't take the bank that `ab.0.1.1` frees (in the trace after it waits for a semaphore of ScalarE; with 0.73 us more in the first tree it starts while `ab.0.1.1` runs). `up.1.0.0.3` takes it, as its wait at 47.15 in the kernel without a chain shows, and that product starts 0.87 later. The slack of 0.4 near 45 doesn't exist there; the thin place is `up.0.0.1.3`, for whose bank `ab.0.1.2` is done at 47.73 + 0.65 = 48.38, against 48.85: 0.47.

*The tree saves 1.5 us, the new order helps more.* This weighting failed. The order alone makes the kernel slower (243.33), the new list without its trees gives nothing (242.35), and the old place of `down.0.0` under trees loses 0.6 to 0.9 of the 1.5. `ab.0.0.3` did end at 48.91 + 0.68 = 49.6 for the forecast 49.3, and `down.0.0` needs it at 51.06 + 6 x 0.216 = 52.4 for 52.0; but that room of 2.8 us at one step isn't what the order buys, because `up.0.0.1.3`, moved ahead, asks VectorE for its bank at 48.85. The prediction looked at the step that waited, and not at the one that it put in its place. The order pays only where VectorE is early enough for that product, and it is the trees that make it so: each takes 41.58 to 44.36, 2.78 us, where two reduces took 2 x 2.09 by starts (41.12 to 43.21 before), so 1.4 us and not 1.5.

*The tree of batch 3.* Right in its times: `qn.2.1` done at 66.33 + 2.34 = 68.7 for 68.6, the two `ab` done at 75.05 for 75.0, `up.0.1.1.2` at 75.80 for 75.7. But that product doesn't wait for these two `ab`: in the trace after it waits for no semaphore of VectorE. With only the tree of batch 2 they end 1.2 us later, and the one wait for an `ab` comes at 83.5 and is 0.24 us.

*From there to down.2.0, slack 0.2.* Wrong in size, and right in its outcome by luck. Both sums were too short: TensorE took 100.55 - 75.80 = 24.75 us for 23.7 (the sum left out `up.0.1.1.2` itself), VectorE 100.91 - 75.05 = 25.86 for 23.5 (0.81 of it idle; eight reduces over q and not seven, and two copies). Held against the start of `down.2.0`, as the prediction did, `ab.2.0.7` is 0.36 us late (100.23 + 0.68 = 100.91 against 100.55). It is needed only for the last matmul, 7 x 0.216 later, at 102.06, so the room is 1.15 us. The prediction counted the matmuls that lie ahead of the late one in `down.0.0`, and forgot them here; 0.73 us more in the second tree cost nothing.

*The price of 0.2 for thin slacks* wasn't paid. The sum without it is 242.07 - 1.23 = 240.84, and 240.61 was measured; the 0.23 between them is less than the spread of the runs (240.45 to 241.06).

*SP's queue, the rows of w3* cost nothing here: TensorE waits for no load and no transpose after 43 us.

*The rivals.* "The room goes" needed VectorE to idle again between `up.0.1.1.2` and `down.2.0`. It did, for 0.81 us, and lost nothing by it, because the room was 1.15 and not 0.2. "The chain makes VectorE wait" needed `qn.2.1` to end after 70.8; its last product waited 0.75 us for its reciprocal (the row at 66.33), where the rival took 2.3 for each of two. The trace after shows no wait of VectorE for GpSimd at any of the five places. The mechanism is real in the old list, where the tree of batch 2 is chained behind `ksub.1.1` and the kernel is slower by 4.5 us. "The change does nothing" fell with the wait.

*The rule on two SBUF inputs.* The Trainium skill (SBUF — State Buffer, Who interferes with whom) says that whichever engine issues first holds the shared port for its whole instruction and the other is blocked. The trace agrees in the unchained kernels that the two block each other, mostly with VectorE as the one that is blocked (6.26 us for 1.22, 2.99 for 0.69, 2.44 for 0.42), and once with both (GpSimd's 5.57 for 4.20). The 6.26 us are more than one instruction's worth, though: they span two of GpSimd's. The prediction named the other side, GpSimd's loss of 2.79 us to the tree; under the chain it came as a wait of 2.37 us before `ksub.1.1`.

## What to carry to other kernels

When a wait is to be removed by putting other work ahead of it, ask of each step put ahead what it waits for in turn; here the order alone only moved VectorE's shortage, and it took less work of VectorE ahead of that step to end it. Cheaper steps that contend with another engine needed both the right place in the list and a chain to hold it: the trees alone lost 4.5 us, the order alone 1.0, the new list without a chain 3.8, and together they gain 1.5. A product of several matmuls waits for its last operand only at its last matmul, so count its room from there. Which product takes a bank that comes free has to be read from the trace; two of the prediction's three slacks were held against the wrong product.

## What the runs showed beside

A long wait of TensorE costs more than itself. After 3.87 us the clock granted for the next 3 us was 0.50; after waits of 1.0 us or less it stayed at 1.00 in the stretches around them. The Trainium skill (TensorE: Matmul & The Clock Gate, Part 1: The HAM clock gate) says that the clock halves after an idle window of about 3.4 us and comes back after as long a busy one; the trace agrees.

In the kernel with unchained trees, a VectorE step that had begun under a GpSimd step didn't get through in the gap between two of them: the second `ksub` at 43.91 started 0.74 us after the end of the first (40.54 + 2.63 = 43.17), and the step still ended only after both. GpSimd issued a load in that gap; whether that kept the step out is not shown.

The start of `up.0.0.0.2` moved by 0.6 us between kernels with the same start, with the landing of `k.0`. Differences of that size in one profile say nothing of a list.
